# Turning probabilities on VectorE and through DRAM, sums spread two to a period, squares in PSUM

## The chip, the cores and the metric

One NeuronCore of a Trainium2 chip runs the whole kernel as a single program. The metric is the device time of one execution in microseconds (us). The engines work in parallel, each through its own list of instructions in order: TensorE (PE, matmuls and its weight loads PEld), VectorE (DVE), ScalarE (ACT), GpSimd (POOL) and SyncE (SP, which issues most of the DMA transfers).

## The reference

Two layers follow each other, all in float32. First an attention in which each query sees the keys within 16 positions and one summary of every block of 32 keys (the maximum of the keys, the mean of the values):

```
B, H, S, D = 4, 8, 768, 64;  block, window = 32, 16;  nb = S // block
k_sum = k.reshape(B, H, nb, block, D).max(axis=3)
v_sum = v.reshape(B, H, nb, block, D).mean(axis=3)
scores_l = where(|i - j| < window, scale * q @ k^T, -1e9)
scores_s = scale * q @ k_sum^T + log(block)
a = softmax(concat([scores_l, scores_s], -1))          # sum + 1e-9 below
x = (a @ concat([v, v_sum], 2)), heads side by side    # 3072 x 512
```

Then a layer with a rational activation, w_in 512 x 2048 and w_out 2048 x 512:

```
h = x @ w_in
P = a[0] + a[1]*h + a[2]*h^2 + a[3]*h^3
Q = 1 + |b[0]|*|h| + |b[1]|*h^2
out = (P / (Q + 1e-6)) @ w_out
```

## The kernel before

The 3072 tokens are cut into 6 groups of 512 (`NG`), the 2048 hidden features into 16 blocks of 128 (`NFC`). A step is one block of one group; there are 96 steps, and the second layer of a step runs three steps behind its first (`LAG`). In each step PE computes h with 12 matmuls into a PSUM bank (`moe1`, L377): weights and x are each split into a high and a low part, and three of the four products are used. ACT and DVE then form the activation (`gelu`, L389): ACT takes the square of h (L400), its absolute value and a linear term; DVE joins square and absolute value (L404); ACT forms the reciprocal by a logarithm and an exponential; DVE and POOL make gh and gl, the two parts of the result. The second layer (`moe2`, L416) takes them in 12 more matmuls into four banks (`po`).

Attention goes in halves of 64 queries, 48 of them (`NHALF`), eight to a group of 512. A half has 120 keys: 96 of its window and 24 summaries. The first eight are computed before step 0, the next eight within steps 0 to 13, whose order is written out by hand (`STEP`, L53). From step 14 on (`NSTRICT`) two halves start every fourth step, at 14, 18, ..., 74: such four steps are called a period here. In that part only PE keeps the order of the text; the order on the other engines and on SP is found by a planner that simulates the program and looks at given priorities (`tc.high_priority`).

A pair of halves passes through these stations. Step s: scores of both on PE (`both_scores`, L195) into two banks of the pool `ps_a`, which has two buffers; then in `scores` (L206) DVE adds the mask and takes the maximum, ACT takes exponentials with their sums, DVE the reciprocal, POOL scales (L240). The probabilities `ss` then lie with queries on partitions. Values need keys on partitions, so PE transposes the four 128x120 blocks of the first half in step s+2 and of the second in step s+3, one ahead of each quarter of the second layer (`turned`, L254; L419 and L420), again into `ps_a`, and ACT copies them to SBUF (`copied`, L292). In step s+4 `both_values` (L297) multiplies them with the values and writes x for the first layer. Right behind stand the scores of the next pair.

SP issues, per half, the loads of values (L246), queries (L187) and keys (L188), besides weights, outputs (L433) and the keys and values for the summaries (L138, L151). The summaries of a batch are formed by DVE (`key_sum`, `value_sum`): four of keys and four of values per batch, one in each of eight steps in a row, which begin 11 steps ahead of the batch's first half (L525 to L533); each load stands one step ahead of its sum.

Of the kernel before, what the change touches and what calls it, by code (L numbers as in the profile page):

```python
# [8 lines left out]
F32 = mybir.dt.float32  # L9
# [3 lines left out]
AF = mybir.ActivationFunctionType  # L13
ALU = mybir.AluOpType
# [4 lines left out]
B, H, S, D = 4, 8, 768, 64  # L19
# [3 lines left out]
P = 128  # L23
NPAIR = H // 2
NCC = DM // P
NFC = DFF // P
HQ = 64
# [2 lines left out]
NKW = HQ + 2 * WIN  # L30
NK = NKW + NB
NKC = NK // NB
GT = 512
NG = NT // GT
HPG = GT // HQ
# [14 lines left out]
NSTG = 8  # L50
EARLY_HALF = (0, 1, 3, 4, 6, 7, 9, 10)
NSTRICT = NFC - 2
STEP = "h3 k0 h0 l0 a0 g1 h1 w2 h1 g1 h3 h0 g0 q0 w2 u g0 q0 w3 g1 h0 w2 w3 P2 v h2"  # L53
NHALF = NT // HQ

# [2 lines left out]
def tile_kernel(ctx, tc, qw_in, kraw, kwin, vpad, vred, wio, a, b, cmask, cident, cavg, out):  # L58
# [147 lines left out]
    def scores(jj, early=False, sc=None):  # L206

        bi, j = divmod(jj, NJ)
        kt, qt = kw[jj % 2], qw[jj % 2] if jj >= HPG else qres[:, jj]
        mt = mask[:, 0 if j == 0 else (2 if j == NJ - 1 else 1), :]  # L210
        ready = sc is not None
        if not ready:
            sc = ps_o.tile([P, 512], F32, tag="o", name=f"sc{jj}") if early else ps_a.tile([P, 512], F32, tag="a", name=f"sc{jj}")
        for pr in range(0 if ready else NPAIR):
            if jj >= HPG:
                keys = ((0, NK, kt[:, :, pr, :]),)
            else:
                keys = ((0, NKW, kres[:, pr, j * HQ:j * HQ + NKW]), (NKW, NK, ksum[0][:, pr, :]))
            for lo, hi, k in keys:
                for e in range(2):  # L220
                    rows = slice(e * D, (e + 1) * D)
                    pe.matmul(sc[rows, pr * NK + lo:pr * NK + hi], qt[rows, pr, :], k[rows], start=True, stop=True)
        yield
        pool, tag = (gp, "gl") if early and jj % 2 else (pp, "p")
        ss = pool.tile([P, NPAIR, NK], F32, tag=tag, name=f"ss{jj}")
        sm = sp.tile([P, 2, NPAIR], F32, tag="sm", name=f"sm{jj}")
        for pr in range(NPAIR):
            dve.tensor_tensor_reduce(
                out=ss[:, pr, :], in0=sc[:, pr * NK:(pr + 1) * NK], in1=mt, op0=ALU.add, op1=ALU.min,
                scale=-SCALE, scalar=3.0e38, accum_out=sm[:, 0, pr:pr + 1])  # L230
        yield
        for pr in range(NPAIR):
            act.activation(ss[:, pr, :], ss[:, pr, :], AF.Exp, scale=-1.0,
                           bias=sm[:, 0, pr:pr + 1], accum_out=sm[:, 1, pr:pr + 1])
        act.activation(sm[:, 1, :], sm[:, 1, :], AF.Copy, bias=1e-9)
        yield
        dve.reciprocal(sm[:, 1, :], sm[:, 1, :])
        yield
        for pr in range(NPAIR):
            gps.tensor_scalar(ss[:, pr, :], ss[:, pr, :], sm[:, 1, pr:pr + 1], 1.0, op0=ALU.mult, op1=ALU.mult)  # L240
        att[jj] = ss

    def load_v(jj):
# [10 lines left out]
    def turned(jj, early=False):  # L254
        pt = ps_h.tile([P, 512], F32, tag="h", name=f"pt{jj}") if early else ps_a.tile([P, 512], F32, tag="a", name=f"pt{jj}")
        for pr in range(NPAIR):
            pe.transpose(out=pt[:NK, pr * P:(pr + 1) * P], in_=att[jj][:, pr, :], identity=ident)
            if pr == NPAIR - 1:
                att[jj] = pt
            yield  # L260
# [28 lines left out]
            yield  # L289
            dve.tensor_tensor(xl[:, :, cols], av, xh[:, :, cols], op=ALU.subtract)  # L290

    def copied(jj):  # L292
        pt = att[jj]
        att[jj] = pp.tile([NK, NPAIR, P], F32, tag="p", name=f"pts{jj}")
        act.copy(att[jj], pt[:NK, :].rearrange("k (r q) -> k r q", r=NPAIR))

    def both_values(j0):  # L297

        g, hh = divmod(j0, HPG)
        if hh == 0:  # L300
            x32[g] = xp.tile([P, NCC, GT], F32, tag="x", name=f"x{g}")
        av = ps_h.tile([P, NPAIR, 2, HQ], F32, tag="h", name=f"av{j0}")
        for k in range(2):
            pts = att.pop(j0 + k)
            for pr in range(NPAIR):
                for e in range(2):
                    pe.matmul(
                        av[e * D:(e + 1) * D, pr, k, :],
                        vw[k][:, (2 * pr + e) * D:(2 * pr + e + 1) * D],
                        pts[:, pr, (e ^ k) * HQ:(e ^ k) * HQ + HQ], start=True, stop=True)  # L310
        act.copy(x32[g][:, :, hh * HQ:(hh + 2) * HQ], av.rearrange("p r k q -> p r (k q)"))

    def split(g):
# [75 lines left out]
    def gelu(h, gh, gl, g, fc):  # L389
        ta = mp.tile([P, GT], F32, tag="ta", name=f"ta{g}_{fc}")  # L390
        tq = mp.tile([P, GT], F32, tag="tq", name=f"tq{g}_{fc}")
        tu = mp.tile([P, GT], F32, tag="tu", name=f"tu{g}_{fc}")
        def products():
            dve.tensor_tensor(tu, tu, h, op=ALU.mult)
            yield
            dve.scalar_tensor_tensor(out=tu, in0=tu, scalar=cs[:, 1:2], in1=h, op0=ALU.add, op1=ALU.mult)


        prods[g * NFC + fc] = products()
        act.activation(tq, h, AF.Square)  # L400
        act.activation(ta, h, AF.Abs, scale=cs[:, 4:5])
        act.activation(tu, h, AF.Identity, scale=cs[:, 3:4], bias=cs[:, 2:3])
        yield
        dve.scalar_tensor_tensor(out=tq, in0=tq, scalar=cs[:, 5:6], in1=ta, op0=ALU.mult, op1=ALU.add)  # L404
        yield
        act.activation(ta, tq, AF.Ln, bias=cs[:, 7:8])
        act.activation(ta, ta, AF.Exp, scale=-1.0)
        yield
        lead(prods.pop(g * NFC + fc), True)
        dve.scalar_tensor_tensor(out=gh, in0=tu, scalar=cs[:, 0:1], in1=ta, op0=ALU.add, op1=ALU.mult)  # L410
        dve.scalar_tensor_tensor(out=tq, in0=tq, scalar=C1 * SH, in1=gh, op0=ALU.add, op1=ALU.mult)
        dve.scalar_tensor_tensor(out=tu, in0=tu, scalar=cs[:, 0:1], in1=tq, op0=ALU.add, op1=ALU.subtract)
        yield
        gps.tensor_tensor(gl, tu, ta, op=ALU.mult)

    def moe2(fc, po, gh, gl, between):  # L416
        wt = weights(fc)
        for t in range(TPG):
            with tc.high_priority(offset=40):  # L419
                next(between, None)  # L420
            ts_ = slice(t * P, (t + 1) * P)
            for i, (l, r) in enumerate(((gh, 0), (gh, 1), (gl, 0))):
                pe.matmul(po[t], l[:, ts_], wt[:, r, 1, :], start=(fc == 0 and i == 0),
                   stop=(fc == NFC - 1 and i == 2))
# [10 lines left out]
    def second_layer(step, queue, po, pt):  # L435
# [6 lines left out]
                finish(g, po)  # L442
        return po

    vnext = tc.dram_tile([NB, DM], F32, name="vnext")
    vres = vw + [mp.tile([NK, DM], F32, tag=t, name=f"vr{i}") for i, t in enumerate(("ta", "tq", "ta", "tq"))]
    vlast = stage.tile([NK, 2, DM], F32, tag="st", name="vlast")
# [28 lines left out]
    def lead(chain, all_of=False):  # L476
        for _ in chain or ():
            if not all_of:
                return
# [2 lines left out]
        lead(turned(jj, early), True)  # L482
        return values(jj, early, copy)

    def turned_copied(jj):
        yield from turned(jj)
        copied(jj)

    def whole(jj):
        yield from scores(jj)  # L490
        yield
# [27 lines left out]
    def start_of(jj):  # L519
        return EARLY_HALF[jj - HPG] if jj < 2 * HPG else NFC - 2 + 4 * ((jj - 2 * HPG) // 2)  # L520
# [3 lines left out]
        halves.setdefault(start_of(jj), []).append(jj)  # L524
    reduces, loads = {}, {}  # L525
    for bi in range(1, B):
        s = max(start_of(bi * NJ) - SOFF, 0)
        for k in range(NPAIR):
            reduces.setdefault(s + k + 1, []).append((key_sum, bi, k))
            loads.setdefault(s + k, []).append((key_load, bi, k))  # L530
        for k in range(NVC if bi > 1 else 0):
            reduces.setdefault(s + NPAIR + k + 1, []).append((value_sum, bi, k))
            loads.setdefault(s + NPAIR + k, []).append((value_load, bi, k))  # L533

    queue, po, x, gelus = [], None, None, {}
    for step in range(NG * NFC + LAG):
# [54 lines left out]
        with tc.high_priority(offset=40):  # L591
            if step - 4 >= NFC - 2 and halves.get(step - 4):
                both_values(halves[step - 4][0])
            for jj in halves.get(step, ()):
                key_blocks(jj)
            for jj, sc in zip(halves.get(step, ()), both_scores(halves[step][0]) if step in halves else ()):
                lead(scores(jj, sc=sc), True)
            for jj in halves.get(step, ()):
                load_v(jj)
                if jj + 2 < NHALF:  # L600
                    att_load(jj + 2)
        pt = (z for k in range(2) for jj in halves.get(step - 2 - k, ())[k:k + 1] if jj >= 2 * HPG for z in turned_copied(jj))
        po = second_layer(step, queue, po, pt)
        with tc.high_priority(offset=40):
            lead(pt, True)
        for f, *args in reduces.get(step, []) + loads.get(step, []):
            f(*args)

# [55 lines left out]
```

## Time and profile before

| | us |
|---|---|
| median of 3 runs (lowest, highest) | 663.37 (661.9, 663.97) |
| the profiled execution | 665.48 |
| its span, first to last instruction | 663.7 |
| PE busy | 643.1 (97%) |
| DVE busy | 573.5 (86%) |
| ACT busy | 475.2 (72%) |
| POOL busy | 272.6 (41%) |

The profile is of one execution; what lies outside its span (1.8 us) is start and end of the program. Busy time is the time in which an engine has an instruction under way. PE's matmuls overlap each other, so the sum of their durations is more than its busy time. A group of rows gives operation, output and inputs by the names in the program, the shapes, the number of instructions, their busy time in us and the mean in ns, then the idle time ahead of them and what ended it. The helper that records the order has line 85, so most rows show L85 and are told apart by their tiles.

### The profile page before, as it was taken

What the parts mean: (1) busy time and instruction counts of PE and PEld (TensorE: products, weight loads), DVE (VectorE), ACT (ScalarE), POOL (GpSimd) and SP (SyncE); (2) the same over time, 40 slices, a digit from 0 to 9 for tenths busy, and PEclk for the clock granted to TensorE, in tenths of its full rate; (3) what the DMA queues carried; (4) which work ended last, traced back from release to release, by engine and by line L of the source; (5) the groups of instructions that cost most, each with busy time, mean ns of one, the idle gap of its engine ahead of it and who ended that gap; (6) DMA issues with size and microseconds to landing.
All of it is one profiled execution on the core that took longest, in us unless ns stands there. A gap on an engine that the chain in (4) does not pass through costs nothing.

```text
span 663.7 us, 11872 instructions
## 1 busy us (share of the span) xinstructions
PE 643.1 (97%) x4196; PEld 509.9 (77%) x4196; DVE 573.5 (86%) x1116; ACT 475.2 (72%) x1068; POOL 272.6 (41%) x318
## 2 busy tenths in 40 slices
PE   8897979999999999999999999999999999999997
PEld 5664757776778788788788788788888788888886
DVE  4579999998989998978889998888888887988885
ACT  3879888977777677787667677678687576665652
POOL 1737557655333354443333343443532442222221
PEclk8989979999999999999999999999999999999999
DMA  9986752502124322122024232012032000010001
GB/s 329 333 294 225 237 176 99 191 24 88 57 96 136 84 76 71 44 85 65 25 65 134 66 112 70 5 61 64 1 127 65 0 25 1 1 64 1 0 1 64
DMA packets 29671, 60.75 MB, mean 92 GB/s; under 512 B 3636, under 2 KB 15284, under 8 KB 27692
## 3 DMA queue, kind: packets, MB, share of 16 engines
q1 hardware_dynamic: 28908, 59.54, 27.6%
q8 instruction: 33, 0.54, 0.3%
q10 hardware_dynamic: 576, 0.25, 0.1%
q14 instruction: 26, 0.21, 0.1%
q0 software_dynamic: 128, 0.20, 0.1%
HBM read 53.44 MB, written 6.34 MB: 90 GB/s over the span
## 4 chain that ended last, share of the span: by engine, by line
PE 80%; DVE 8%; DMA 4%; ACT 3%; issue 3%; POOL 1%; SPq 0%; DVEq 0%; ACTq 0%
PE po L85 36%; PE h L85 34%; PE sc L85 4%; PE av L85 3%; DMA wr<-in_wio_dram 3%; PE pt L85 2%; DVE tu L85 2%; DVE tq L85 2%; DVE wr L85 1%; ACT ta L85 1%; DMA kres<-in_kraw_dram 1%; POOL ss L85 1%; DVE gh L85 1%; DVE ss L85 1%; PE vf L85 1%
## 5 line engine op out<-in xcount | busy, mean ns | idle before, releaser
L85 POOL TENSOR_TENSOR gl<-tu,ta 128x512 fp32r<-128x512 f32 x96 | 134.5, 1401 | 269.5 <-DVE tu L85 175.0
L85 POOL TENSOR_SCALAR ss<-ss,sm 128x120 f32<-128x120 f32 x192 | 110.2, 592 | 105.9 <-DVE sm L85 103.3
L85 PE MATMUL po<-wearly,gh 128*128 128x512 f32 x384 | 130.2, 421 | 0.0
L85 PE MATMUL po<-w,gh 128*128 128x512 f32 x384 | 126.7, 411 | 0.0
L85 DVE SCALAR_TENSOR_TENSOR tq<-tq,cs,ta 128x512 f32<-128x512 f32 x96 | 101.5, 1058 | 28.3 <-ACT ta L85 27.9
L85 ACT ACTIVATE tq<-h 128x512 f32<-128x512 f32 x96 | 57.1, 595 | 82.7 <-PE h L85 80.0
L85 ACT ACTIVATE ta<-tq,cs 128x512 f32<-128x512 f32 x96 | 69.6, 725 | 60.5 <-DVE tq L85 59.9
L85 PE MATMUL h<-xh,wearly 128*128 128x512 f32 x384 | 97.5, 395 | 1.7 <-DVE tu L85 1.2
L85 PE MATMUL h<-xh,w 128*128 128x512 f32 x384 | 95.1, 390 | 0.0
L85 DVE SCALAR_TENSOR_TENSOR gh<-tu,cs,ta 128x512 fp32r<-128x512 f32 x96 | 78.1, 813 | 15.8 <-ACT ta L85 9.8
L85 PEld LDWEIGHTS h<-xh,wearly 128*128 128x128 f32 x384 | 71.7, 188 | 20.7 <-ACT xh L85 2.0
L85 PEld LDWEIGHTS h<-xh,w 128*128 128x128 f32 x384 | 72.1, 188 | 15.5
L85 ACT ACTIVATE ss<-ss,sm 128x120 f32<-128x120 f32 x192 | 73.3, 385 | 12.8 <-DVE sm L85 12.4
L85 PEld LDWEIGHTS po<-wearly,gh 128*128 128x128 f32 x384 | 66.1, 193 | 18.1 <-issue 2.6
L85 PEld LDWEIGHTS po<-w,gh 128*128 128x128 f32 x384 | 66.0, 189 | 16.9 <-issue 1.3
L85 PE MATMUL po<-w,gl 128*128 128x512 f32 x192 | 75.4, 393 | 1.0 <-POOL gl L85 1.0
L85 PE MATMUL po<-wearly,gl 128*128 128x512 f32 x192 | 76.3, 397 | 0.0
L85 DVE SCALAR_TENSOR_TENSOR tu<-tu,cs,tq 128x512 f32<-128x512 f32 x96 | 72.8, 758 | 2.7
L85 ACT ACTIVATE tu<-h,cs 128x512 f32<-128x512 f32 x96 | 74.9, 780 | 0.0
L85 DVE SCALAR_TENSOR_TENSOR tu<-tu,cs,h 128x512 f32<-128x512 f32 x96 | 71.6, 745 | 2.6
L85 DVE SCALAR_TENSOR_TENSOR tq<-tq,gh 128x512 f32<-128x512 f32 x96 | 69.6, 725 | 3.2
L85 ACT ACTIVATE ta<-h,cs 128x512 f32<-128x512 f32 x96 | 65.5, 683 | 5.8 <-POOL gl L85 5.7
(68 smaller groups left out, 947.6 us busy)
## 6 DMA issues: line engine op xcount, KB each, us to landing
wr<-in_wio_dram SPq DMA_DIRECT2D x15, 1024.0 KB, 6.3
vw<-in_vpad_dram SPq DMA_DIRECT2D x42, 192.0 KB, 2.7
kw<-in_kwin_dram SPq DMA_DIRECT2D x40, 192.0 KB, 3.5
out_dram<-o SPq DMA_DIRECT2D x24, 256.0 KB, 2.1
qw<-in_qw_dram SPq DMA_DIRECT2D x40, 128.0 KB, 2.9
kr<-in_kraw_dram SPq DMA_DIRECT2D x12, 384.0 KB, 3.1
vr<-in_vred_dram SPq DMA_DIRECT2D x8, 384.0 KB, 3.4
vf<-in_vpad_dram SPq DMA_DIRECT2D x2, 1024.0 KB, 12.1
```

What stands on the lines that cost most here:

```text
L85: out = getattr(self.engine, name)(*args, **kw)
```

## The change

Four things change. (1) From the 17th half on, PE no longer transposes. `crossed` takes the place of `turned` and `copied`: DVE transposes the 32x32 blocks of `ss` within themselves, the result is written to a tile in DRAM, and four transfers bring it back with the blocks in their new places. For that `ss` is widened from 120 to 128 columns, and POOL sets the added ones to zero. `both_values` reads the new layout. `crossed` stands in the text one step behind the scores. (2) The two halves of a pair go through `scores` station by station instead of one after the other. (3) In steps 15 to 77, those that start a pair of halves excepted, the square of h goes to a bank of `ps_a` instead of SBUF. (4) The sums for the third and fourth batch are placed at the third and fourth step of a period (not at a group's first step, step 16 excepted), two to a period; their loads stand two sums ahead. The second batch's keep their places.

```diff
+SQ = 32
+NKB = -(-NK // SQ)
+CROSS = 1
...
-        ss = pool.tile([P, NPAIR, NK], F32, tag=tag, name=f"ss{jj}")
+        ss = pool.tile([P, NPAIR, P], F32, tag=tag, name=f"ss{jj}")[:, :, 0:NK if jj < 2 * HPG else P]
...
+        if jj >= 2 * HPG:
+            gps.memset(ss[:, :, NK:], 0.0)
...
-    def copied(jj):
-        pt = att[jj]
-        att[jj] = pp.tile([NK, NPAIR, P], F32, tag="p", name=f"pts{jj}")
-        act.copy(att[jj], pt[:NK, :].rearrange("k (r q) -> k r q", r=NPAIR))
+    def crossed(jj):
+
+        ss = att[jj]
+        tu = pp.tile([P, NKB, NPAIR, SQ], F32, tag="p", name=f"tb{jj}")
+        dve.transpose(out=tu.rearrange("p n r q -> p r n q"), in_=ss.rearrange("p r (n q) -> p r n q", q=SQ))
+        nc.sync.dma_start(out=cross[jj % 4], in_=tu)
+        att[jj] = pp.tile([NK, P // SQ, NPAIR, SQ], F32, tag="pts", name=f"pts{jj}", bufs=2)
+        for n in range(NKB):
+            k = min(SQ, NK - n * SQ)
+            nc.sync.dma_start(
+                out=att[jj][n * SQ:n * SQ + k],
+                in_=cross[jj % 4][:, n].rearrange("(b a) r q -> a b r q", a=SQ)[0:k])
...
-                        pts[:, pr, (e ^ k) * HQ:(e ^ k) * HQ + HQ], start=True, stop=True)
+                        pts[:, 2 * (e ^ k):2 * (e ^ k) + 2, pr, :], start=True, stop=True)
...
-        act.activation(tq, h, AF.Square)
+        sq = tq
+        if NSTRICT < g * NFC + fc < start_of(NHALF - 1) + 4 and (g * NFC + fc) not in halves:
+            sq = ps_a.tile([P, GT], F32, tag="a", name=f"sq{g}_{fc}")
+        act.activation(sq, h, AF.Square)
...
-        dve.scalar_tensor_tensor(out=tq, in0=tq, scalar=cs[:, 5:6], in1=ta, op0=ALU.mult, op1=ALU.add)
+        dve.scalar_tensor_tensor(out=tq, in0=sq, scalar=cs[:, 5:6], in1=ta, op0=ALU.mult, op1=ALU.add)
...
+    cross = [tc.dram_tile([P, NKB, NPAIR, SQ], F32, name=f"cross{i}") for i in range(4)]
...
-        s = max(start_of(bi * NJ) - SOFF, 0)
-        for k in range(NPAIR):
-            reduces.setdefault(s + k + 1, []).append((key_sum, bi, k))
-            loads.setdefault(s + k, []).append((key_load, bi, k))
...
+        end = start_of(bi * NJ)
+        sums_of = [(key_load, key_sum, k) for k in range(NPAIR)] + [(value_load, value_sum, k) for k in range(NVC if bi > 1 else 0)]
+
+        places = [t for t in range(max(end - 22, NFC), end) if t % 4 < 2 and (t == NFC or t % NFC)][-len(sums_of):] if bi > 1 else range(1, 5)
+        for i, (t, (load, add, k)) in enumerate(zip(places, sums_of)):
+            reduces.setdefault(t, []).append((add, bi, k))
+            loads.setdefault(t - 1 if bi == 1 else places[i - 2] if i > 1 else t - 3, []).append((load, bi, k))
...
-            for jj, sc in zip(halves.get(step, ()), both_scores(halves[step][0]) if step in halves else ()):
-                lead(scores(jj, sc=sc), True)
+            if step in halves:
+                chain = [scores(jj, sc=sc) for jj, sc in zip(halves[step], both_scores(halves[step][0]))]
+            else:
+                chain = ()
+            for _ in range(5):
+                for c in chain:
+                    lead(c)
+            for jj in halves.get(step - CROSS, ()):
+                if jj >= 2 * HPG:
+                    crossed(jj)
...
-        pt = (z for k in range(2) for jj in halves.get(step - 2 - k, ())[k:k + 1] if jj >= 2 * HPG for z in turned_copied(jj))
-        po = second_layer(step, queue, po, pt)
-        with tc.high_priority(offset=40):
-            lead(pt, True)
+        po = second_layer(step, queue, po, None)
```

## Rows read from the trace of the kernel before

**Rows 1.** The page, busy us of each engine, share of the span, instructions:

```profile
PE 643.1 (97%) x4196; PEld 509.9 (77%) x4196; DVE 573.5 (86%) x1116; ACT 475.2 (72%) x1068; POOL 272.6 (41%) x318
```

**Rows 2.** Table by stretches: busy us (instructions) of each engine, clock, DMA:

```profile
core 0: us, PE busy (x) PEld busy (x) DVE busy (x) ACT busy (x) POOL busy (x), PEclk, DMA share, GB/s
...
180.00:540.00 360.00, 359.39 (x2383) 289.33 (x2382) 316.13 (x648) 263.86 (x626) 144.52 (x178) 1.00 0.23 70
340.00:380.00 40.00, 39.39 (x261) 31.35 (x260) 37.82 (x66) 27.95 (x60) 13.88 (x15) 1.00 0.29 86
```

**Rows 3.** The page, the chain that ended last, share of the span by engine:

```profile
PE 80%; DVE 8%; DMA 4%; ACT 3%; issue 3%; POOL 1%; SPq 0%; DVEq 0%; ACTq 0%
```

**Rows 4.** Timeline of PE, one period: start us, length us, engine, line, operation:

```profile
429.26 1.15 PE L85 MATMUL av<-pts,vw 120*64 120x64 f32 x32
...
434.18 1.98 PE L85 MATMUL h<-xh,w 128*128 128x512 f32 x8
...
439.62 1.98 PE L85 MATMUL h<-xh,w 128*128 128x512 f32 x8
...
445.60 2.01 PE L85 MATMUL h<-xh,w 128*128 128x512 f32 x8
...
451.60 1.98 PE L85 MATMUL h<-xh,w 128*128 128x512 f32 x8
...
454.41 1.15 PE L85 MATMUL av<-pts,vw 120*64 120x64 f32 x32
```

**Rows 5.** The tile pt from 158 to 560 us: count, ns min/median/max, starts:

```profile
L85 PE MATMUL pt<-ident,ss x128: 269/271/274, 161.9 to 551.4; 128*120 128x128 f32 x128
L85 ACT COPY pts<-pt x32: 562/567/590, 167.5 to 552.0; 120x512 f32<-120x512 f32 x32
```

**Rows 6.** Groups of instructions by form, whole span: count, busy us, mean ns:

```profile
L85 DVE SCALAR_TENSOR_TENSOR tq<-tq,cs,ta 128x512 f32<-128x512 f32 x96 | 101.5, 1058 | 28.3 <-ACT ta L85 27.9
...
L85 DVE SCALAR_TENSOR_TENSOR tu<-tu,cs,h 128x512 f32<-128x512 f32 x96 | 71.6, 745 | 2.6
...
L85 ACT ACTIVATE tq<-h 128x512 f32<-128x512 f32 x96 | 57.1, 595 | 82.7 <-PE h L85 80.0 <-DVE tu L85 1.6 <-issue 1.0
...
L85 DVE TENSOR_REDUCE ks<-kr 128x24 f32<-128x768 f32 x12 | 11.3, 942 | 0.0
...
L85 DVE COPY pts<-pt 120x512 f32<-120x512 f32 x5 | 3.4, 682 | 0.8 <-PE pt L85 0.8
```

**Rows 7.** Timeline, DVE and POOL at work together, two places:

```profile
430.29 1.27 POOL L85 TENSOR_TENSOR gl<-tu,ta 128x512 fp32r<-128x512 f32 x1 [3.07 <-DVE tu L85]
...
430.57 1.53 DVE L85 SCALAR_TENSOR_TENSOR tq<-tq,cs,ta 128x512 f32<-128x512 f32 x1 [0.46 <-ACT ta L85]
...
444.19 1.65 POOL L85 TENSOR_TENSOR gl<-tu,ta 128x512 fp32r<-128x512 f32 x1 [1.50 <-DVE tu L85]
...
444.60 0.68 DVE L85 TENSOR_TENSOR tu<-tu,h 128x512 f32<-128x512 f32 x1
```

**Rows 8.** Timeline of PE and POOL: a late period's values and scalings, a usual period's scalings:

```profile
227.28 1.15 PE L85 MATMUL av<-pts,vw 120*64 120x64 f32 x32
...
238.41 4.82 POOL L85 TENSOR_SCALAR ss<-ss,sm 128x120 f32<-128x120 f32 x8
...
437.27 3.72 POOL L85 TENSOR_SCALAR ss<-ss,sm 128x120 f32<-128x120 f32 x8 [5.71 <-DVE sm L85]
```

**Rows 9.** The page, DMA issues (count, KB, us to landing); timeline of SP, one issue:

```profile
kw<-in_kwin_dram SPq DMA_DIRECT2D x40, 192.0 KB, 3.5
out_dram<-o SPq DMA_DIRECT2D x24, 256.0 KB, 2.1
...
431.82 0.42 SPq L188 DMA_DIRECT2D kw<-in_kwin_dram  x1
```

**Rows 10.** Timeline of PE, steps 16 and 17, with the wait ahead in brackets:

```profile
163.57 0.51 PE L85 MATMUL po<-w,gl 128*128 128x512 f32 x1 [0.96 <-POOL gl L85]
...
167.65 2.12 PE L85 MATMUL h<-xh,wearly 128*128 128x512 f32 x8 [1.16 <-DVE tu L85]
```

**Rows 11.** Waits of SP's queue from 180 to 560 us: total, times, longest:

```profile
SPq L138 <- DVE ks L85: 28.2, 4, 10.8
```

More of the change, by code (lines that the diff above doesn't have):

```diff
@@ L228, in scores @@
             dve.tensor_tensor_reduce(
-                out=ss[:, pr, :], in0=sc[:, pr * NK:(pr + 1) * NK], in1=mt, op0=ALU.add, op1=ALU.min,
+                out=ss[:, pr, 0:NK], in0=sc[:, pr * NK:(pr + 1) * NK], in1=mt, op0=ALU.add, op1=ALU.min,
                 scale=-SCALE, scalar=3.0e38, accum_out=sm[:, 0, pr:pr + 1])
@@ L232, in scores @@
         for pr in range(NPAIR):
-            act.activation(ss[:, pr, :], ss[:, pr, :], AF.Exp, scale=-1.0,
+            act.activation(ss[:, pr, 0:NK], ss[:, pr, 0:NK], AF.Exp, scale=-1.0,
                            bias=sm[:, 0, pr:pr + 1], accum_out=sm[:, 1, pr:pr + 1])
@@ L238, in scores @@
         yield
+        if jj >= 2 * HPG:
+            gps.memset(ss[:, :, NK:], 0.0)
         for pr in range(NPAIR):
-            gps.tensor_scalar(ss[:, pr, :], ss[:, pr, :], sm[:, 1, pr:pr + 1], 1.0, op0=ALU.mult, op1=ALU.mult)
+            gps.tensor_scalar(ss[:, pr, 0:NK], ss[:, pr, 0:NK], sm[:, 1, pr:pr + 1], 1.0, op0=ALU.mult, op1=ALU.mult)
         att[jj] = ss
@@ L307, in both_values @@
                     pe.matmul(
-                        av[e * D:(e + 1) * D, pr, k, :],
+                        av[e * D:(e + 1) * D, pr, k, :].rearrange("d (b q) -> d b q", q=SQ),
                         vw[k][:, (2 * pr + e) * D:(2 * pr + e + 1) * D],
-                        pts[:, pr, (e ^ k) * HQ:(e ^ k) * HQ + HQ], start=True, stop=True)
+                        pts[:, 2 * (e ^ k):2 * (e ^ k) + 2, pr, :], start=True, stop=True)
         act.copy(x32[g][:, :, hh * HQ:(hh + 2) * HQ], av.rearrange("p r k q -> p r (k q)"))
@@ L419, in moe2 @@
             with tc.high_priority(offset=40):
-                next(between, None)
+                lead(between)
             ts_ = slice(t * P, (t + 1) * P)
@@ L483, in finish_half @@
         return values(jj, early, copy)
-    def turned_copied(jj):
-        yield from turned(jj)
-        copied(jj)
     def whole(jj):
@@ L526, in tile_kernel @@
     for bi in range(1, B):
-        s = max(start_of(bi * NJ) - SOFF, 0)
-        for k in range(NPAIR):
-            reduces.setdefault(s + k + 1, []).append((key_sum, bi, k))
-            loads.setdefault(s + k, []).append((key_load, bi, k))
-        for k in range(NVC if bi > 1 else 0):
-            reduces.setdefault(s + NPAIR + k + 1, []).append((value_sum, bi, k))
-            loads.setdefault(s + NPAIR + k, []).append((value_load, bi, k))
+        end = start_of(bi * NJ)
[4 more added lines that the diff above has]
+            loads.setdefault(t - 1 if bi == 1 else places[i - 2] if i > 1 else t - 3, []).append((load, bi, k))
     queue, po, x, gelus = [], None, None, {}
```

## The prediction

> **What bounds the kernel now.** I read the page's engine totals first: TensorE (PE) is busy 97% of the span, VectorE (DVE) 86%, ScalarE (ACT) 72%, GpSimd (POOL) 41% [rows 1]. An average hides stages, so the table by stretches came next: from 180 to 540 us, where the attention of the later batches runs between the layers, PE is busy 359.39 of 360.00 us at a granted clock of 1.00 (the 2.4 GHz level) and DVE 316.13 [rows 2]. The chain that ended last is PE for 80% [rows 3]. So a microsecond taken off PE there is a microsecond of the result, unless something else is then late; one taken off another engine is nothing.
>
> The order of PE's work in one period of four steps gives the price of each piece [rows 4]. First-layer groups of a step start at 434.18, 439.62, 445.60 and 451.60 us, and values (av) of one pair of halves at 429.26, of the next at 454.41: a period is 25.15 us. The step without attention takes 439.62 - 434.18 = 5.44 us, the two with four transposes each 5.98 and 6.00. Eight transposes therefore cost 0.54 + 0.56 = 1.10 us of a period. (Their own row says 271 ns each [rows 5], but they overlap their neighbours; what counts is how much the step grows.) In the rest, 25.15 - 4 x 5.44 - 1.10 = 2.29 us, are values and scores, which stay.
>
> **Part 1, transposes leave PE.** 128 go, in 16 periods, and with them 32 copies of 567 ns on ACT [rows 5]. PE: 16 x 1.10 = 17.6 us off the path. ACT's 18.1 us come off an engine that ends nothing here: nothing gained. The new period, if PE keeps its cover, is 25.15 - 1.10 = 24.05 us.
>
> **Part 2, the same turning on DVE.** Each half gets one DVE transpose of 128x512 in 32x32 blocks, two per period. The trace has none. Below: a one-source reduction of 768 columns takes 942 ns, so 512 columns scale to 0.63 us; the copy of as many columns out of PSUM takes 682 ns [rows 6]. Above: a DVE operation that meets POOL at work took 1.53 us [rows 7]. I take 0.68 us, since it is one source and one pass as the copy is. Per period +1.36 us (1.26 to 3.06).
>
> **Part 3, squares in PSUM.** The DVE operation that reads the square (tq<-tq,cs,ta) has a mean of 1058 ns, while its like with h from PSUM (tu<-tu,cs,h) has 745 [rows 6]. Why is seen where POOL works: the first took 1.53 us beside POOL's product at 430.29, whereas an operation with an operand in PSUM took 0.68 us beside a POOL product at 444.19, and there it was POOL that took longer, 1.65 us for 1.27 [rows 7]. With the square in PSUM in three of four steps (48 in all), DVE saves up to 3 x 0.31 = 0.94 us a period; at worst nothing. I take 0.94. ACT's squaring (595 ns [rows 6]) has slack either way. The square takes turns in the bank pair that scores use. Scores of step s+4 thus wait for DVE to have read the square of step s+3: from the end of h(s+3) PE still has a second layer, a first layer and the values, 2.7 + 2.7 + 1.15 = 6.6 us, and ACT and DVE need some 0.6 + 0.7 + 0.75 to 1.53 us. It costs only if DVE lags by 4 us.
>
> DVE in sum: 316.13 / 360 x 25.15 = 22.08 us a period [rows 2], + 1.36 - 0.94 = 22.5 of 24.05, 94%. Before it stood at 88%, and at 37.82 of 40 from 340 to 380 us, where PE still had 39.39 [rows 2]. Gelu's results are used three steps later, 16 us, so a full DVE for one period is bridged. It fits, narrowly.
>
> The Trainium skill bears on this ("SBUF — State Buffer", Who interferes with whom): a DVE instruction with at most one SBUF input, outside the two-port modes, does not contend with GpSimd. The pair of operations above agrees (0.68 against 1.53 us); no run here shows it for a transpose. By the rule DVE stays at 22.5 us; without it, by the 1.53 us row, it is 24.2.
>
> **Part 4, the transfers.** Each half adds a 256 KB write to DRAM and four reads back, all on SP: ten issues of up to 0.42 us per period [rows 9], 4.2 us of SP's time, beside six issues now. Nothing on SP is busy, but it works in order. A write waits for DVE, a read for the landing of its write; behind them stand the next values, queries and keys (not wanted before the next period), output stores (nobody waits soon) and the loads for the sums. The question is whether the turned probabilities are there when PE comes to the values, 24.05 us after the previous ones. In the usual period POOL's scaling ends at 437.27 + 3.72, 11.7 us after its values started, the first half 1.9 us earlier (half of eight operations) [rows 4, 8]. First transpose done at 9.9 + 0.68 = 10.5; its write, by the output store of the same size, lands 2.1 us later [rows 9], 12.6; its four reads are issued until 14.3; the second write behind them lands at 16.4; the last of its four reads is issued at 17.7 and lands, by the 3.5 us of a load of the keys [rows 9], at 21.2. Slack 2.9 us. If the second write goes out ahead of the first reads, it is nearly 5. In the latest period (values at 227.28, scaling ends at 243.23, 16.0 us [rows 8]) the same sum ends at 25.5: 1.4 us late, or in time with the better order; and that period held sums of keys and values which now move to its other steps. I cost the transfers at nothing, with 1 us late in a period or two as the high end.
>
> The row says 2.1 us for a 256 KB write to DRAM. The Trainium skill ("DMA: Bandwidth & Descriptors", Anatomy of one DMA) speaks against a trip through HBM: about 2.0 us fixed plus bytes over 436 GB/s, and the write's receipt can take surprisingly long there. By it each write is 2.6 us (an estimate from that page) and the usual period ends 1.0 us later, still in time.
>
> **Part 5, sums and small things.** The number of sums is the same, so DVE's total is; they are spread to the two steps of a period that have no scores. That should lift the crowding at 340 to 380 us (0.6 us of PE [rows 2]). But for the third batch they now begin at steps 16 and 17, where PE already waits: 0.96 us for POOL and 1.16 for DVE [rows 10], while the second group's input is split. Two key sums of 0.94 us [rows 6] fall into it. Between 0 and 1.9 us lost, and I take the whole 1.9 since DVE is the late one there. The zeroing on POOL is less than a scaling operation of 0.46 us [rows 8] and can run early; halves in lockstep change the order of text, not the work. The first 14 steps and the last 100 us keep their work.
>
> **Sum.** -17.6 + 1.9 = -15.7 us on the profiled execution's 665.48 (span 663.7): 649.8. The median of the runs shown is 2.1 us below that execution, so 663.37 - 15.7 = 647.7.
>
> **Rivals.**
> DVE becomes the bound. For it: 94% after the change, and POOL shares something with it [rows 7]. Against: the transpose has one source, squares leave that conflict. If transposes are blocked (+3.06) and squares gain nothing, DVE needs 25.1 us a period and the whole gain is lost. Midway the period is 24.6: 16 x 0.55 = 8.8 off, 654.6. This case spans 652 to 663.
>
> The round trip becomes the loop (the slower side). Its place is PE's wait before the values; it decides from the point where the way from one pair's values to the next takes over 25.15 us, 4.0 above my 21.2. For it: two transfers in series, SP in order, behind loads that wait for sums (28.2 us in 4 waits [rows 11]), a scaling that can end at 16.0 us. Against: 3 to 5 us of slack in the usual period. With writes that land like a load of the keys (2 x 1.4 more) and blocked transposes (2 x 0.85) the usual period needs 25.7 us and the latest 30.0; the usual one alone costs 16 x 0.55 = 8.8 us, 674, and a quarter of the way to the latest 690.
>
> **How the numbers follow.** The forecast has 0.63; its own range is 643.7 (17.6 off, and the 2.1 us of waits of [rows 10] too) to 652 (2 us more lost at steps 16 to 18 and 2 in late periods). DVE as the bound 0.19, of which 0.04 ends within 0.3%. The round trip 0.18, of which 0.03 ends within 0.3%. About 0.3%, 2 us, is what a measurement of this kernel can tell from no change. Faster 0.63 + 0.15 = 0.78, same 0.07, slower 0.15. The range goes from 643 to 662, to the end of DVE's case, and leaves out the round trip.
>
> **What would show it.** Right: periods of 24.05 us between the starts of values, no transposes or copies on PE and ACT after 160 us, PE still at 99% from 180 us on, DVE transposes near 0.68 us, the operation on squares near 0.75 us, reads landed 3 us ahead of the values. Wrong: PE idle in front of av, released by a transfer (the round trip); DVE above 97% and PE idle in front of po, waiting for gh or gl (DVE); periods still at 25.15; a wait for squares in front of scores.

## The result, and the profile after

The changed kernel takes 654.72 us (median of 4 runs, 653.99 to 656.37) against 663.22 us (4 runs) for the kernel before: ratio 0.9875, 95% interval [0.9853, 0.9897]. That is faster, as forecast, inside the range of 643 to 662 us, but half of the gain: 8.5 us instead of 15.7.

The page of the kernel after, engine totals and the chain that ended last (beside [rows 1, 3]):

```profile
PE 627.3 (96%) x4068; PEld 499.4 (76%) x4068; DVE 577.2 (88%) x1148; ACT 460.4 (70%) x1036; POOL 258.9 (40%) x350
...
PE 60%; DVE 19%; ACT 9%; POOL 4%; issue 4%; DMA 2%; SPq 0%; DVEq 0%; POOLq 0%; ACTq 0%
```

PE has lost 16 us of work, but it is no longer alone on the chain: its share fell from 80% to 60%, and DVE's rose from 8% to 19%.

The starts of the values mark the periods. In a calm one the timeline of PE shows exactly what was forecast, 544.51 - 520.46 = 24.05 us, with first layers 5.44 us apart and no transposes (beside [rows 4]):

```profile
520.46 1.15 PE L88 MATMUL av<-pts,vw 120*64 120x64 f32 x32
525.38 1.98 PE L88 MATMUL h<-xh,w 128*128 128x512 f32 x8
530.82 1.98 PE L88 MATMUL h<-xh,w 128*128 128x512 f32 x8
536.26 1.98 PE L88 MATMUL h<-xh,w 128*128 128x512 f32 x8
541.70 1.98 PE L88 MATMUL h<-xh,w 128*128 128x512 f32 x8
544.51 1.15 PE L88 MATMUL av<-pts,vw 120*64 120x64 f32 x32
```

But of the 15 periods from the first to the last of these values only seven take under 24.1 us. The others take 24.43 to 26.62 us. I call the sum over 15 x 24.05 us the lateness: 544.51 - 173.03 - 360.75 = 10.7 us. The table by stretches, one period to a row and all of them in the last (columns as in [rows 2], the ends of most rows rounded), shows three calm ones, the second, the fourth and the ninth:

```profile
323.20:347.20 24.00, 24.00 (x161) 19.75 (x160) 22.17 (x47) 16.54 (x39) 8.47 (x14) 1.00 0.38 120
197.88:224.52 26.64, 24.24 (x161) 19.71 (x160) 24.90 (x49) 18.00 (x42) 10.17 (x16) 1.00 0.36 113
224.52:248.60 24.08, 24.07 (x162) 19.80 (x162) 22.62 (x49) 15.03 (x37) 8.42 (x13) 1.00 0.43 131
248.60:274.70 26.10, 24.96 (x163) 19.57 (x162) 24.97 (x50) 18.60 (x44) 11.60 (x16) 1.00 0.31 99
373.17:399.01 25.84, 24.64 (x160) 19.62 (x160) 23.01 (x49) 18.22 (x43) 8.40 (x14) 1.00 0.42 138
423.10:447.10 24.00, 24.00 (x161) 19.75 (x160) 20.57 (x45) 16.67 (x39) 8.58 (x14) 1.00 0.28 87
173.03:544.51 371.48, 364.04 (x2401) 295.70 (x2400) 334.71 (x699) 261.11 (x613) 138.41 (x214) 1.00 0.35 110
```

The third busy time is DVE's. In the calm periods shown it has 20.57 to 22.62 us of work, and PE is busy throughout; the second row has three sums and 24.90 us, the fourth a split (a new group's x cut into its two parts) and 24.97 us, more than PE's own 24.05. Those two periods last as long as DVE's work and 1.1 to 1.7 us of its waits. But DVE's total is not the whole cause: only the second, the fourth and the eighth (24.32 us) have more than 24.05 us of DVE's work, and they make 6.5 of the 10.7 us. The ninth, in the fifth row, takes 25.84 us with 23.01 us of it, and the first 24.88 with 22.45.

The timeline around the longest wait of PE (columns as in [rows 4], the wait ahead and its releaser in brackets):

```profile
218.29 0.75 DVE L88 SCALAR_TENSOR_TENSOR tu<-tu,cs,h 128x512 f32<-128x512 f32 x1
...
221.05 1.08 PE L88 MATMUL h<-xl,w 128*128 128x512 f32 x4
...
221.89 1.21 DVE L88 TENSOR_REDUCE vs<-vr 96x32 f32<-96x1024 f32 x1
...
223.02 0.68 DVE L88 TENSOR_TENSOR tu<-tu,h 128x512 f32<-128x512 f32 x1
...
223.73 0.75 DVE L88 SCALAR_TENSOR_TENSOR tu<-tu,cs,h 128x512 f32<-128x512 f32 x1
...
224.53 1.15 PE L88 MATMUL av<-pts,vw 120*64 120x64 f32 x32 [2.40 <-DVE tu L88]
```

PE has finished h of step 26 at 222.1 and wants to write the values, but their bank is that of h of step 25 (the pool of h has two buffers, and the values take turns in it). DVE reads that h last at 223.73 to 224.48, so it is done 7.9 us after PE had finished that h at 216.6; a sum stood ahead of it. (That it is step 25's was counted: it is the 26th such operation of the trace.) PE does not wait for transfers, nor for gh or gl.

All waits of PE from 173 to 545 us (total, times, longest):

```profile
PE av L88 <- DVE tu L88: 4.1, 4, 2.4
PE h L88 <- DVE tu L88: 1.8, 3, 0.9
PE po L88 <- ACT o L88: 1.2, 2, 1.0
PE h L88 <- DVE xl L88: 0.2, 1, 0.2
```

The first two rows, 5.9 us, are waits for banks of h; in the second one an h waits until DVE has read the h of two steps before. Both waits for ACT's copies of the output lie in the ninth period. All waits together are 371.48 - 364.04 = 7.4 of the 10.7 us. The other 3.3 us stand in PE's busy time, 364.04 us against 360.75; 0.65 us of it is there without transposes on DVE too (next section), and what fills the rest is open.

### The profile page after: what moved, and what is told of

The parts are those of the page before. It is cut to its first block, busy times and chain, and to the rows that moved or that the text cites. A ratio compares the mean times of both kernels' runs of the same rounds, so it can differ in the third digit from the quotient of the medians.

```text
span 653.1 us, 11832 instructions
## 1 busy us (share of the span) xinstructions
PE 627.3 (96%) x4068; PEld 499.4 (76%) x4068; DVE 577.2 (88%) x1148; ACT 460.4 (70%) x1036; POOL 258.9 (40%) x350
## 4 chain that ended last, share of the span: by engine, by line
PE 60%; DVE 19%; ACT 9%; POOL 4%; issue 4%; DMA 2%; SPq 0%; DVEq 0%; POOLq 0%; ACTq 0%
PE po L88 27%; PE h L88 25%; DVE tu L88 6%; DVE tq L88 5%; PE sc L88 3%; POOL ss L88 3%; ACT ss L88 3%; DVE gh L88 3%; PE av L88 3%; ACT ta L88 2%; POOL gl L88 1%; DVE ss L88 1%; PE pt L88 1%; DMA kres<-in_kraw_dram 1%; PE vf L88 1%
## 5 line engine op out<-in xcount | busy, mean ns | idle before, releaser
L88 POOL TENSOR_TENSOR gl<-tu,ta 128x512 fp32r<-128x512 f32 x96 | 129.7, 1351 | 291.1 <-DVE tu L88 169.9
L88 POOL TENSOR_SCALAR ss<-ss,sm 128x120 f32<-128x120 f32 x192 | 98.6, 535 | 89.7 <-DVE sm L88 89.5
L88 PE MATMUL po<-wearly,gh 128*128 128x512 f32 x384 | 125.2, 408 | 1.4 <-ACT o L88 1.2
L88 PE MATMUL po<-w,gh 128*128 128x512 f32 x384 | 120.3, 394 | 0.0
L88 PEld LDWEIGHTS po<-wearly,gh 128*128 128x128 f32 x384 | 71.2, 193 | 19.4 <-ACT o L88 3.1
L88 PEld LDWEIGHTS h<-xh,w 128*128 128x128 f32 x384 | 72.0, 188 | 15.2 <-DVE tu L88 0.2
L88 PEld LDWEIGHTS po<-w,gh 128*128 128x128 f32 x384 | 70.8, 188 | 15.7 <-issue 1.3
L88 DVE SCALAR_TENSOR_TENSOR gh<-tu,cs,ta 128x512 fp32r<-128x512 f32 x96 | 73.8, 769 | 9.5 <-ACT ta L88 1.8
L88 DVE TENSOR_TENSOR tu<-tu,h 128x512 f32<-128x512 f32 x96 | 64.9, 676 | 0.0
L88 DVE SCALAR_TENSOR_TENSOR tq<-tq,cs,ta 128x512 f32<-128x512 f32 x48 | 54.7, 1141 | 9.0 <-ACT ta L88 8.6
```

The source lines that it names most:

```text
L88: out = getattr(self.engine, name)(*args, **kw)
```

## The experiments

Theory DVE: PE waits where DVE has more to do than a period lasts; the transfers land in time. Rival: the way through DRAM is late. Beside each median and its ratio to the kernel before on the same chip stand two readings of its profile: the start of step 13's first layer, up to which all run the same steps, and the lateness of the 15 periods over 24.05 us.

| run | median us | ratio [95%] | start of step 13 | lateness |
|---|---|---|---|---|
| before | 663.22 | | 152.54 | 17.7 |
| after | 654.72 | 0.9875 [0.9853, 0.9897] | 149.71 | 10.7 |
| after, again | 656.69 | 0.9898 [0.9866, 0.9930] | 151.32 | 10.7 |
| no trip through DRAM | 658.08 | 0.9918 [0.9902, 0.9933] | 152.71 | 11.1 |
| no transposes on DVE | 647.65 | 0.9754 [0.9738, 0.9771] | 151.40 | 0.8 |
| sums of one in 32 | 651.13 | 0.9800 [0.9779, 0.9821] | 151.16 | 5.3 |
| squares in SBUF | 661.33 | 0.9962 [0.9937, 0.9987] | 149.77 | 15.2 |
| PE transposes, sums and lockstep new | 663.52 | 0.9972 [0.9942, 1.0002] | 148.90 | 17.3 |
| sums in a row | 658.11 | 0.9891 [0.9836, 0.9946] | 149.02 | 13.6 |
| sums two steps on | 655.94 | 0.9878 [0.9808, 0.9949] | 148.60 | 11.9 |
| sums of values on POOL | 663.09 | 0.9968 [0.9939, 0.9998] | 150.89 | 17.3 |
| sums where there is room | 656.84 | 0.9886 [0.9844, 0.9928] | 153.08 | 10.7 |
| that, a quarter of a split on POOL | 659.38 | 0.9934 [0.9907, 0.9960] | 151.12 | 14.8 |
| PE transposes in four full periods | 655.39 | 0.9859 [0.9825, 0.9894] | 156.08 | 8.8 |

**No trip through DRAM.**

```diff
-        nc.sync.dma_start(out=cross[jj % 4], in_=tu)
-        att[jj] = pp.tile([NK, P // SQ, NPAIR, SQ], F32, tag="pts", name=f"pts{jj}", bufs=2)
...
+        att[jj] = tu[0:NK]
```

> Leaves out the trip through DRAM: the values read the tile that DVE has transposed, with its blocks in their old places. Theory DVE (PE waits where DVE has more to do than a period lasts; the transfers land in time): 653 to 656 us, the long periods stay near 26 us. Rival round trip (the waits ahead of the values are for landings): those waits go, about 6 us, 648 to 649 us.

The median, 658.08, lies above the changed kernel's and above both expectations; the periods don't show it. They are the same one by one (24.95, 26.60, 24.07, 26.01 against 24.88, 26.62, 24.05, 26.07 us for the first four), and so are PE's waits from 173 to 545 us:

```profile
PE av L88 <- DVE tu L88: 4.2, 4, 2.4
PE h L88 <- DVE tu L88: 1.7, 3, 0.9
PE po L88 <- ACT o L88: 1.2, 2, 1.0
PE h L88 <- DVE xl L88: 0.2, 1, 0.2
```

The 160 transfers cost nothing; the rival falls. Of the 4.7 us by which this profile's span is longer, 3.0 lie ahead of step 13, where nothing was edited (last section), and 1.3 behind the last values.

**No transposes on DVE.**

```diff
-        tu = pp.tile([P, NKB, NPAIR, SQ], F32, tag="p", name=f"tb{jj}")
-        dve.transpose(out=tu.rearrange("p n r q -> p r n q"), in_=ss.rearrange("p r (n q) -> p r n q", q=SQ))
-        nc.sync.dma_start(out=cross[jj % 4], in_=tu)
+        nc.sync.dma_start(out=cross[jj % 4].rearrange("p n r q -> p (n r q)"), in_=ss.rearrange("p r k -> p (r k)"))
```

> Leaves out the 32 transposes on DVE: the scaled probabilities themselves go to DRAM and come back by the same transfers. Theory DVE: 32 x 0.71 = 22.7 us less on DVE, 8 of the 10.7 us of late periods go, 646 to 649 us. Rival round trip: each transfer starts only 0.7 us earlier, 652 to 655 us.

647.65 us, lateness 0.8: without transposes on DVE nearly the whole 1.10 us a period arrives. From its first to its last values PE is busy 361.40 of 361.51 us:

```profile
176.18:537.69 361.51, 361.40 (x2401) 296.59 (x2401) 320.05 (x666) 261.84 (x612) 134.36 (x212) 1.00 0.36 113
```

DVE is still busy 320.05 / 361.51 = 89% there, and 23.17 us in the fourth period, which takes 24.05. The step from no lateness to 10 us is small in DVE's share: 334.71 / 371.48 = 90% in the changed kernel.

**Sums of one in 32.** Key sums of the third and fourth batch and value sums read `[:, :, 0:1]` of each block.

> The sums of the third and fourth batch read one key or value of each block of 32 instead of all; loads, waits and order stay. Theory DVE: 16 operations of 0.95 to 1.21 us shrink to some 0.2, 14 us less on DVE, all in the periods from 173 to 420 us; those without a split fall to 24.1 to 24.5 us, 649 to 651 us. Rival round trip: 653 to 656 us.

651.13 us. The second period falls from 26.62 to 24.11 us, the ninth from 25.84 to 24.36, the third is 24.05 either way; the split periods, fourth, eighth and twelfth, come to 24.98, 25.01 and 24.81, from 26.07, 25.94 and 24.86. So of the 10.7 us some 5.4 come from the sums. Of what is left, 2.6 us lie in the three splits and 2.5 in the periods with output copies (first, fifth, ninth and thirteenth). The first misses the expectation: it rose from 24.88 to 25.47 us with 1.2 us less of DVE's work, and why is open.

**Squares in SBUF.**

```diff
-        if NSTRICT < g * NFC + fc < start_of(NHALF - 1) + 4 and (g * NFC + fc) not in halves:
-            sq = ps_a.tile([P, GT], F32, tag="a", name=f"sq{g}_{fc}")
```

> Undoes one part: all squares of h stay in SBUF. Theory DVE: the operation on squares goes back from 0.74 to some 1.1 us in 48 steps, 15 to 19 us more on DVE; periods with room swallow it, full ones don't: 658 to 662 us. If the squares are worth nothing, 653 to 656 us.

661.33 us, lateness 15.2: the time was as expected, and the squares in PSUM are worth some 4.5 us of the change. DVE's work was not. Over all 96 steps the operation on squares takes 94.6 us here against 35.5 + 54.7 = 90.2 in the changed kernel (48 operations each, rows in the next section), 4.4 us more instead of 15 to 19. POOL pays more: its busy time rises from 258.9 to 272.0 us.

```profile
L88 DVE SCALAR_TENSOR_TENSOR tq<-tq,cs,ta 128x512 f32<-128x512 f32 x96 | 94.6, 985 | 11.6 <-ACT ta L88 11.1
```

**PE transposes, sums and lockstep new.** The kernel before, with the new places of the sums and the two halves station by station.

> The kernel before with two parts of the change alone: halves in lockstep and the sums in their new places; PE still transposes, squares stay in SBUF. Both theories: PE is the bound at 25.15 us a period and neither part takes anything off it, 661 to 664 us. If the places of the sums or the lockstep were worth something by themselves, under 660 us.

663.52 us, the interval includes no change, and all periods but two take 25.14 to 25.16 us (25.32 and 25.79). Neither part is worth anything that shows while PE is the bound.

**Sums in a row.** The changed kernel with the places and loads of before.

> Undoes one part: the sums of the third and fourth batch stand in eight steps in a row again. Theory DVE by its total: the same work, in fewer periods; lateness of the 15 periods stays at 9 to 13 us, 654 to 657 us. If spreading them was what kept DVE in time, over 658 us.

658.11 us and lateness 13.6, both just above what the theory by DVE's total gives; 27.44, 25.88 and 25.59 us in the first three periods and 27.92 in the eighth. By the periods spreading is worth about 3 us here, and nothing in the run before, where PE is the bound; the times do not tell this run from the changed kernel (the interval [0.9836, 0.9946] holds its ratio). DVE's total alone does not decide: it is 332.0 us in the 15 periods, less than the changed kernel's 334.7.

**Sums two steps on.**

```diff
+        places = {1: range(1, 5), 2: (17, 18, 19, 22, 23, 26, 27, 28), 3: (35, 38, 39, 42, 43, 47, 50, 51)}[bi]
```

> Moves the sums two steps in the text, to the first two steps of a period, since DVE came to them some 10 us after PE's step, right ahead of the work on scores; steps whose sums would meet a split are left out. If the place counts: two to four of the 8 us of DVE's lateness go, 651 to 653 us. If only DVE's total in a period counts: 654 to 656 us.

655.94 us, lateness 11.9: a miss for the place. The second period went from 26.62 to 24.84, but the first rose to 28.20, where DVE now had three key sums instead of two (176.01, 185.66 and 189.01 us), the last two among the transposes.

**Sums of values on POOL.**

```diff
-        tc.keep_in_program_order(dve.tensor_reduce(vs[:, c, :], vr, axis=AX.X, op=ALU.add))
+        n = BLK // 2
+        while n > 1:
+            gps.tensor_tensor(vr[:, :, 0:n], vr[:, :, 0:n], vr[:, :, n:2 * n], op=ALU.add)
+            n //= 2
+        gps.tensor_tensor(vs[:, c, :], vr[:, :, 0], vr[:, :, 1], op=ALU.add)
```

> The eight sums of values are added up on POOL by halves (5 additions each) instead of by DVE. Theory DVE: 8 x 1.21 = 9.7 us less on DVE in the periods from 200 to 420 us, 651 to 653 us. Rival: POOL's reads hold up DVE's operations with two SBUF inputs by as much (1.53 us against 0.74 was seen), 654 to 657 us.

Worse than either expectation, 663.09 us, lateness 17.3. DVE's 9.7 us went, but its total fell only by 6.3 us (577.2 to 570.9). POOL got 31.3 us for them (32 additions of 855 ns on average and 8 of 496 ns), DVE's transposes waited 18.6 us for POOL's scaling instead of 12.7, and in the second period alone PE waited twice for DVE's reading of h:

```profile
217.63 3.11 PE L88 MATMUL h<-xh,w 128*128 128x512 f32 x8 [2.58 <-DVE tu L88]
...
229.77 0.45 PE L88 MATMUL av<-pts,vw 120*64 120x64 f32 x8 [2.06 <-DVE tu L88]
```

**After, again.**

> The changed kernel once more, for the start: of the 10.6 us between the first two profiles 2.8 lie before step 13, where nothing was changed. If the start belongs to the kernel, its first-layer group of step 13 begins near 149.7 us again and the median is 654 to 656 us; if it varies by itself, it begins anywhere from 148.6 to 152.7 us, as it did in the other runs. Either way the 15 periods are late by 10 to 12 us.

656.69 us; the start differs by 1.6 us from the first profile, the 15 periods by at most 0.03 us each. The start varies by itself.

**Sums where there is room, and a quarter of a split on POOL.**

```diff
+        places = {1: range(1, 5), 2: (16, 17, 20, 21, 25, 26, 28, 29), 3: (33, 34, 36, 37, 40, 41, 43, 44)}[bi]
```

> Moves the sums of the fourth batch into the three periods ahead of the split in which DVE had 1.9 to 2.9 us to spare (text steps 33 to 44), and of the third batch's one from the second period into the third. Theory DVE by the room of each period: the last two late periods lose 2 to 2.5 us, the second 1, lateness 7 to 8.5 us, 651 to 653 us. If lateness only moves: 654 to 656 us.

656.84 us, lateness 10.7 again: a miss. The ninth period fell to 24.05 and the eighth to 24.98, the second to 25.49, but the fourth, fifth and seventh rose to 26.75, 25.49 and 25.65. The second run adds this:

```diff
-            dve.tensor_tensor(xl[:, c], x32[g][:, c], xh[:, c], op=ALU.subtract)
+            (gps if c > 2 else dve).tensor_tensor(xl[:, c], x32[g][:, c], xh[:, c], op=ALU.subtract)
```

> As the run with the sums in the periods that have room, and one of the four subtractions of a split on POOL: DVE has 0.87 us less in each of the three split periods. If DVE's work is all: 0.5 to 1 us less in each, 1.5 to 3 us below that run. Rival: POOL is scaling probabilities then, the fourth part comes late and PE waits for it: 1 to 3 us above that run.

659.38 us, 2.5 us above that run, and 4.2 us more lateness: the rival. The fourth period takes 31.16 us and the twelfth 27.93, where PE waits for the fourth part behind POOL's scaling:

```profile
266.71 0.79 PE L88 MATMUL h<-xl,wearly 128*128 128x512 f32 x1 [3.29 <-POOL ss L88]
```

**PE transposes in four full periods.** Halves of steps 22, 30, 46 and 50 go through `turned` and `copied` again, and the squares of the three steps behind each stay in SBUF.

> In the four periods that were late by 1.8 to 2.6 us (halves of steps 22, 30, 46, 50) PE transposes again as before and the squares stay in SBUF; the other twelve are as in the changed kernel. Theory DVE by the room of each period: these four take PE's 25.15 to 25.4 us instead of 25.8 to 26.6, lateness over 24.05 us in 15 periods 7 to 9 us instead of 10.7, 652 to 654 us. If lateness only moves to other periods, as when the sums were moved: 10 us or more, 655 to 658 us.

Lateness 8.8, as expected in sum: 25.82, 26.18, 25.14 and 25.14 us in the four instead of 26.62, 26.07, 25.94 and 25.84. Two of them miss the 25.15 to 25.4 us, and the third period rose from 24.05 to 24.81. The time, 655.39 us, does not show it (the interval [0.9825, 0.9894] holds the changed kernel's ratio): its profiled execution came to step 13 3.5 us later than that of before. That this version beats the changed kernel is not shown.

## Why half of the gain came

**Transposes leave PE: right, 17.6 us.** The calm periods take 24.05 us, and the run without DVE's transposes has all 15 of them but for 0.8 us. That its 647.65 us is also the time that I forecast for the changed kernel is partly chance: its profiled start was 1.1 us ahead of that of before.

**DVE's work: the sum was right, and it did not fit.** Groups by form in the kernel after (columns as in [rows 6]):

```profile
L88 DVE SCALAR_TENSOR_TENSOR tq<-tq,cs,ta 128x512 f32<-128x512 f32 x48 | 54.7, 1141 | 9.0 <-ACT ta L88 8.6
...
L88 DVE SCALAR_TENSOR_TENSOR tq<-sq,cs,ta 128x512 f32<-128x512 f32 x48 | 35.5, 740 | 3.8 <-ACT ta L88 3.7
...
L88 DVE STREAM_TRANSPOSE tb<-ss 128x512 f32<-128x512 f32 x32 | 22.7, 709 | 13.0 <-POOL ss L88 12.7
```

The transpose takes 0.71 us (0.68 taken) and was never lengthened by POOL: all 32 lie within 694 to 714 ns, and 21 of them ran wholly beside one of POOL's scalings or products. With that the rule of the Trainium skill ("SBUF — State Buffer", Who interferes with whom) holds here for it, as for the squares (708 to 753 ns).

DVE has 334.71 / 15 = 22.3 us a period; I had worked out 22.5. Part of that is luck: over the 15 periods the operation on squares went from 60.5 to 33.3 + 16.2 us, 0.73 a period instead of 0.94, and gh's operation, which I had left alone, gave another 0.25 (838 to 777 ns). And a mean of 22.3 hid three periods above 24.05.

The step that failed is the sentence on cover: "Gelu's results are used three steps later, 16 us, so a full DVE for one period is bridged." PE does not need gh first. It needs the bank that h lies in: h and the values share two banks, so the values of step s wait until DVE has read h of step s-1. From the end of that h PE has its own second and first layer to do, 2.7 + 2.7 us, and then waits. The cover is 5.4 us, not 16; at 224 us DVE was done 7.9 us after PE, and the wait was 2.4. I had done this sum for the bank of the scores, and not for that of h. Waits for banks of h are 5.9 of the 10.7 us. This is read from the trace; no run gave the values a bank of their own.

The second thing missed stands in the last of these rows: the transposes made DVE wait 12.7 us for POOL's scaling, in 15 of 32 cases. The change put an operation at the head of DVE's queue whose input comes from POOL, and gelu's operations, ready or not, stood behind. I named what waits behind SP's transfers and not what waits behind this. What that costs is not shown: 6.7 of the 12.7 us lie in the seven calm periods, where nothing was late. The run without transposes takes away 22.7 us of work and this wait together; which part of its 9.9 us less lateness belongs to which is open.

**Squares: right per operation, too large in sum.** 1058 to 740 ns, 48 times, would be 15 us of DVE. But the 48 squares left in SBUF rose to 1141 ns, so all 96 went from 101.5 to 90.2 us, 11.3 less; against the run with all squares in SBUF it is 4.4 us. In time the squares are worth some 4.5 us.

**Transfers: right.** No landing shows in PE's waits, and the run without the trip has the same periods. SP's rows of one calm period (values at 520.46 and 544.51) end the eight issues of reads at 536.61, 16.2 us after the values, where I had the last one begin at 17.7:

```profile
531.03 1.72 SPq L302 DMA_DIRECT2D cross<-tb  x2
533.07 3.54 SPq L306 DMA_DIRECT2D pts<-cross  x8
```

Both writes went out ahead of the first reads here, the better order of the two; in the late second period they did not. From a write's issue to that of the first read that waits for it took 2.0 us here and at most 3.0 (184.45 to 187.44, in the first period), against 2.1 in the prediction and 2.6 in its estimate from the Trainium skill; the section named there gives its figure for transfers issued by GpSimd, and these are SP's.

**Sums: the place was read from the text.** I expected steps 16 and 17 to lose 1.9 us. The way from step 13 to the first values took 173.03 - 149.71 = 23.3 us instead of 24.1, so 0.8 of the 1.1 us arrived: 0.3 lost. The loss came later. DVE got to the sums of steps 20, 21 and 24 at 200.3, 202.3 and 221.9 us, all in the second period, and that one became the longest.

**The rivals.** PE late by DVE is what happened (19% given), and 654.72 us lies next to the 654.6 named as that case's middle. That is luck: 654.6 stood for transposes held up and squares that gain less, 24.6 us of DVE's work a period, and DVE has 22.3. Nor did its sign come, DVE above 97% and PE idle in front of po: DVE stood at 90%, and PE idled in front of av and h. The forecast itself, 643.7 to 652, missed; the range held because it included this case. (In the sum of the round trip 663.37 + 8.8 is 672, not 674.)

The balance of the two profiles, 663.7 - 653.1 = 10.6 us: 2.8 ahead of step 13, where the two starts had different clocks (last section), 0.7 to the first values, 7.0 of the 16.5 us expected in the 15 periods, and 0.1 after them. By this account the change is worth some 7.7 us.

## What to carry to other kernels

An engine at 88% beside one at 100% is no cover for more work: go through the shared banks and ask how far behind the reader of each may be before the writer stops. The slack is that of the shortest such loop, not of the longest pipeline. And a moved operation brings its wait with it: what stands behind it in the new queue can pay for the input's lateness, even if the operation itself is short (its price was not shown here).

Spread work costs nothing only where the engine has room in that period; where a planner orders the queue, its place is read from the trace, not from the text. Even then the totals by period were a poor guide: sums moved to the periods with room left the lateness at 10.7 us.

## What was not expected of the hardware

How long the start of the kernel takes goes with the clock that TensorE is granted in the first 20 us. The first stretch of three profiles (columns as in [rows 2], the clock third from the end, 1.00 for the 2.4 GHz level throughout): the kernel after, the run without the trip, the run with PE in four periods.

```profile
0.00:20.00 20.00, 17.93 (x186) 10.69 (x188) 9.39 (x53) 9.62 (x43) 4.08 (x16) 1.00 0.93 316
```

```profile
0.00:20.00 20.00, 17.35 (x180) 11.42 (x181) 8.51 (x46) 8.45 (x37) 2.97 (x12) 0.91 0.93 314
```

```profile
0.00:20.00 20.00, 17.41 (x143) 11.41 (x144) 8.29 (x43) 8.59 (x37) 2.97 (x12) 0.79 0.93 314
```

Step 13 began at 149.71, 152.71 and 156.08 us. The other profiles agree: with 1.00 in this stretch it began at 148.6 to 151.4 us, with 0.91 (the kernel before among them) at 152.5 to 153.1. What sets the clock of an execution is not shown. Some 6 us lie between these three, nearly as much as the change is worth, so the kernels were compared by their periods and not by their medians alone.
